# Moving batch 1's sums of q and k from the front of a fused attention and MoE kernel into its first matmul block

## Chip, cores and metric

One core of a Trainium2 chip runs the whole program. The metric is the device time of one execution in microseconds; the number of a kernel is the median of its runs. Each kernel also has one profiled execution, from which all rows below come.

## What is computed

The reference takes q, k and v of shape (4, 8, 576, 64), that is batch, heads, tokens, head size, and two sets of weights. The attention is a dense one on tokens pooled by four (144 of 576) plus one in a band of seven tokens; its result, as 2304 rows of 512, goes through a gated layer (inner width 1536) and a second one (inner width 2048).

```python
q_d = q.reshape(B, H, Sd, factor, D).mean(axis=3)
k_d = k.reshape(B, H, Sd, factor, D).mean(axis=3)
v_d = v.reshape(B, H, Sd, factor, D).mean(axis=3)
out_d = sm_attn(q_d, k_d, v_d)
out_up = np.repeat(out_d, factor, axis=2)
mask = np.abs(pos[:, None] - pos[None, :]) < factor
...
return (out_up + out_local).astype(np.float32)
...
return (silu * val @ w_out).astype(np.float32)
...
g = h * relu6 / 6.0
return (g @ w_out).astype(np.float32)
```

## The kernel before

**Blocks and units.** The 2304 tokens are cut into five blocks (`BLOCKS`, line 30). Block 0 has 512 columns, nearly all of batch 0. A block runs 68 units in a fixed order (line 152 and on): G and V (gate and value products, 12 matmuls each), O (the product with w_out), then H and P of the second layer. Units come in pairs: G0 G1 V0 V1 G2 G3 V2 V3 O0 O1 G4 G5 V4 V5 O2 O3 and so on. A pair shares one tile `wr` of split weights. In the first block the number m of a unit is its place in this list: G2 is m = 4, G5 is m = 11, O3 is m = 15.

**Weights.** In block 0 they come as 64-bit floats, one DMA of 512 KB for a unit on SP's queue (line 219). ScalarE takes the upper bits (`top`, line 236), VectorE joins the rest into fp32 (`w`, line 245), ScalarE and VectorE split that into a high and a low part (`wr`, lines 263 and 268), and ScalarE's queue stores the fp32 pair to DRAM for the later blocks (`kept`, line 251). Four raw buffers rotate, so that SP's next load waits for a line 245 four units back. `prefetch` (line 273) gives each step its lead in units.

**The front.** `first_batch` (line 362) does all of batch 0's attention before the first G, in an order written by hand: the string `FRONT` (line 46), whose words are steps on PE, VectorE and ScalarE.

**Batch 1's sums.** The second block needs batch 1's attention, which runs beside block 0. Its pooled q and k are made by GpSimd (POOL). The last word of `FRONT`, `sums` (line 706), issues four DMAs that load two of four tokens each (q and k, two halves, into the tile `stage`, 288 KB each), then four that add the other two tokens onto them in the DMA (line 702), then four additions (line 716) into `dnq` and `dnk`. `stage` takes over the buffer (tag `x2`) of `held`, the softmax of the front, so the first load waits for the last reader of `held`. `sums_T` (line 329) then transposes dnq and dnk on PE in four steps of four (`pqT_0`, `pqT_1`, `pkT_0`, `pkT_1`, line 336), ScalarE copies each to `qdT` or `kdT` (line 347), and the first dense scores of batch 1 (`pS`) use these in the H units. The loop over units takes one step of this at every odd m above 8 (line 1144).

**Order.** PE, VectorE and ScalarE work off their own lists in order. Program order is not the final order: unless an instruction is pinned, a scheduler may put it elsewhere on its engine. It put `pqT_0`, in the program after unit O1 (m = 9), between G2 and G3.

**Band scores.** `first_half` (line 1096) spreads VectorE's products `pr` (line 839) and their reductions `sc` (line 842) for batch 1's band over the units with m from 0.

Of the kernel before, what the change touches and what calls it, by code (L numbers as in the profile page):

```python
# [11 lines left out]
F32 = mybir.dt.float32  # L12
F32R = mybir.dt.float32r
# [6 lines left out]
ALU = mybir.AluOpType  # L20
AX = mybir.AxisListType

P = 128
# [16 lines left out]

SMALL = 384
SUMV = 25
FILL_P = (4, 4, 4, 4, 4, 0)


# [3 lines left out]
SC0 dM1 M0 Rk3 dE1 Rk2 dT0 dP0 W0 SC1 dS3 dM3 dT1 dP1 SC2 M1 dE3 W1 dS2 dT3 N0 dM2 dP3 SC3 dE2 dT2  # L49
PT0 M2 to0 N1 M3 dP2 to1 de0 Pd0 W3 dO0 dO3 dN0 dN3 dO2 N3 dO1 Pa0 W2 dN2 dN1 to2 PT1 Pa1 Pd1 SC5  # L50
SC4 M5 od0 W5 od1 PT3 V1 M4 N2 Pa3 de1 Xh1 W4 V0 Xh0 Pd3 Xl1 N5 PT2 V3 Pd2 Pa2 Xl0 hi0 PT5 Xh3 N4
Pd5 Pa5 Xl3 to3 V2 Xh2 PT4 de2 Xl2 Pd4 Pa4 de3 V5 lo0 Xh5 V4 Xh4 Xl5 Xl4 hi1 to4 lo1 sums
"""


# [1 line left out]
def tile_kernel(  # L57
# [12 lines left out]
    nc = tc.nc  # L70

    B, H, S, D = q.shape
# [5 lines left out]
    NJH = NJ // 2  # L78
    W = 7
    NC = DM // P  # L80
    F1 = w_gate.shape[1] // P
    F2 = w2_in.shape[1] // P
    UT = 4 * NSEG
# [4 lines left out]
    UMAX = max(BLOCKS)  # L88
# [6 lines left out]
    sp = ctx.enter_context(tc.tile_pool(name="sp", bufs=2))  # L95
# [15 lines left out]
    consts = cp.tile([P, SMALL // 4], F32, name="consts")  # L111
# [65 lines left out]
    NU = len(units) // NB  # L177
    NU1 = 3 * F1
# [133 lines left out]
    dn, qk = {}, {}  # L312

    def down_sums(b, kinds, gate=None):
        if gate is not None:
            tc.keep_in_program_order(nc.gpsimd.tensor_copy(consts[:gate.shape[0], 60:61], gate))
        for ws in kinds:
            for t in range(4):
                for w in ws:
                    if t == 0:  # L320
                        dn[w] = sp.tile([NJH, 2, H, D], F32, tag="dn" + w, name=f"dn{w}{b}", bufs=1)
                    src = {"q": q, "k": k, "v": v}[w]
                    for half in range(2):
                        tok = src[b, :, half * NJH * 4:(half + 1) * NJH * 4, :].rearrange("h (j t) d -> j t h d", t=4)
                        how = {"accum_op": ALU.add} if t else {}
                        tc.keep_in_program_order(nc.gpsimd.dma_start(dn[w][:, half], tok[:, t], **how))
                    yield

    def sums_T(b):
        for w in "qk":  # L330
            for hc in range(2):
                pt = bank("pa", f"p{w}T{b}_{hc}")[:, :2 * NJ].rearrange("p (c j) -> p c j", c=2)
                for cc in range(2):
                    c = 2 * hc + cc
                    for half in range(2):
                        nc.tensor.transpose(
                            pt[:, cc, half * NJH:(half + 1) * NJH],
                            dn[w][:, half, 2 * c:2 * c + 2, :].rearrange("j h d -> j (h d)"),
                            ident[:NJH, :NJH],
                        )  # L340
                yield w, hc, pt
# [20 lines left out]
    def first_batch():  # L362
# [7 lines left out]
        with tc.tile_pool(name="fp", bufs=1) as fp:  # L370
# [5 lines left out]
            first = {  # L376
                "fdpd": fp.tile([NJH, 2, 2, NJ], F32, tag="fdpd", name="fdpd_0", bufs=3),
                "fdpT": fp.tile([NJH, 2, NJ], F32, tag="fdpT", name="fdpT_0", bufs=8),
            }
# [123 lines left out]
            def fill(ps, n):  # L503

                for _ in range(n):
                    pe.matmul(ps[:, :2 * P], spin[:, :P], spin, start=True, stop=True)
# [140 lines left out]
            def PT(i):  # L647
                for hh in range(2):
                    ps = bank(f"acc{2 + hh}", f"fPT{i}_{hh}")
                    if not hh:  # L650
                        fill(ps, FILL_P[i])
                    ps = ps[:WK, :4 * QT].rearrange("p (h s) -> p h s", h=4)
# [35 lines left out]
                    to = columns(bi, col, xv)  # L688
                    vec.tensor_tensor(to[:, :, 1], xv, to[:, :, 0].bitcast(F32), op=ALU.subtract)

            twos = {}

            def pairs(t):
                for w, src in (("q", q), ("k", k)):
                    for half in range(2):
                        if not t:
                            st = stage[0][:, len(twos)]
                            twos[w, half] = st.rearrange("p (h t d) -> p h t d", h=H, t=2)
                        tok = src[1, :, half * NJH * 4:(half + 1) * NJH * 4, :]
                        tok = tok.rearrange("h (j t) d -> j h t d", t=4)[:, :, t:t + 2]  # L700
                        how = {"accum_op": ALU.add} if t else {}
                        tc.keep_in_program_order(nc.gpsimd.dma_start(twos[w, half], tok, **how))

            stage = []

            def sums():
                st = sp.tile([P, NC, 2, UMAX * UT], F32R, tag="x2", name="stage", bufs=1).bitcast(F32)
                stage.append(st.rearrange("p c a t -> p (c a t)")[:NJH].rearrange("p (n e) -> p n e", n=4))
                pairs(0)
                pairs(2)  # L710
                for w in "qk":
                    dn[w] = sp.tile([NJH, 2, H, D], F32, tag="dn" + w, name=f"dn{w}1", bufs=1)
                    for half in range(2):
                        st = twos[w, half]
                        tc.keep_in_program_order(
                            nc.gpsimd.tensor_tensor(dn[w][:, half], st[:, :, 0], st[:, :, 1], op=ALU.add)
                        )

            def od(n):
                for i in ((1, 0), (3, 2, 5, 4))[n]:  # L720
                    join_od(i)
# [11 lines left out]
            def lo(i):  # L733
# [2 lines left out]
            others = {  # L736
                "dS": dS, "dM": dM, "dE": dE, "dT": dT, "dP": dP, "dO": dO,
                "dN": dN, "SC": SC, "M": M, "W": W, "N": N, "PT": PT,
                "Pa": Pa, "Pd": Pd, "V": V, "Xh": Xh, "Xl": Xl, "sums": sums,
                "od": od, "to": to, "de": de, "hi": hi, "lo": lo,  # L740
            }
            for step in FRONT.split():
                name, *arg = re.match(r"([A-Za-z]+?)([qk]?)(\d*)$", step).groups()
                if name in ("T", "E", "R"):
                    w, at = arg
# [107 lines left out]
    def chunk_exp(b, c, n):  # L853
        sc, _ = pes[b, c]

        tc.keep_in_program_order(nc.scalar.activation(sc, sc, AF.Exp, scale=0.125))
# [129 lines left out]
    state = {}  # L986
# [102 lines left out]
    for bi in range(NB):  # L1089
        mine = chunks[at:at + len(CUTS[bi])]  # L1090
        at += len(mine)
        limit = starts[bi + 2] if bi + 2 <= NB else 0

        db = bi + 1 if bi + 1 < B else None

        def first_half():
            for m, ch in enumerate(mine):
                for _ in chunk_scores(*ch):
                    yield
                load_ahead(at - len(mine) + m + 3 if m + 3 <= len(mine) else loaded)  # L1100
            for _ in range(VAL0.get(bi, 0)):
                unit_values()
                yield

        def weigh(ch):
            chunk_exp(*ch)
            vq.extend((*ch, i) for i in range(ch[2]))

        def second_half():
            for ch in mine[1:] if bi in VAL0 else mine:  # L1110
                weigh(ch)
            while vq:
                unit_values()
                yield

        gens = [first_half(), second_half()]
        sizes = [sum(CUTS[bi]) + VAL0.get(bi, 0), sum(CUTS[bi]) - VAL0.get(bi, 0)]
        main = iter(())
        sums = iter(())
        if db:  # L1120
            sums = down_T(db, dn, qk)
            if bi:
                sums = chain(down_sums(db, ["qk", "v"], state["os"][:, (UMAX // 2 - 2) * DM:][:, :1]), sums)
        for i in range(bi * NU, (bi + 1) * NU):
            m = i - bi * NU
            prefetch(i)
            if m in CLOAD:
                load_ahead(at - len(mine) + min(CLOAD.index(m) + 1, len(mine)))
            if m == EXP_AT and bi in VAL0:
                weigh(mine[0])  # L1130
            run_unit(i)
            ph = 0 if m < NU1 else 1
            if m == NU1:
                for _ in gens[0]:
                    pass
                for _ in sums:
                    pass
                if db:
                    main = down_main(db, dn, qk)
            lo_, n_ = (0, NU1 - 2) if ph == 0 else (NU1, NU - NU1 - 6)  # L1140
            mm_ = m - lo_
            for _ in range(sizes[ph] * (mm_ + 1) // n_ - sizes[ph] * mm_ // n_ if mm_ < n_ else 0):
                next(gens[ph], None)
            if m % 2 and (bi or m > 8):
                next(sums, None)
            next(main, None)
            if m == NU - EARLY:
                load_ahead(at + 1)
            if i == SUMV:
                last = [t for key, t in state.items() if key[0] == "g"][-1]  # L1150
                for _ in down_sums(1, ["v"], last[:, 0, :1].bitcast(F32)):
                    pass
            step_x(limit)
            next_tick()
        if bi + 1 < NB:
            for _ in gens[1]:
                pass
            for _ in main:
                next_tick()
            while x_done[0] < starts[bi + 2]:  # L1160
                step_x(limit)
                next_tick()
# [30 lines left out]
```

## Time and profile before

| | us |
|---|---|
| median of 3 runs | 969.19 (968.88 to 971.98) |
| the profiled execution, own time | 970.18 |
| its span, first to last instruction | 968.4 |
| PE busy (matmuls) | 932.7 (96%) |
| VectorE (DVE) busy | 730.6 (75%) |
| ScalarE (ACT) busy | 504.2 (52%) |
| GpSimd (POOL) busy | 105.5 (11%) |

The span is the profiled execution's time from its first to its last instruction. Times in the rows below count from the start of the span. A bracket at the end of a row is the time for which the engine had stood idle before it and what released it. L with a number is the line of the kernel.

### The profile page before, as it was taken

How to read it: one execution, taken by the hardware profiler on the slowest of the kernel's cores; microseconds unless marked ns; L12 is line 12 of the kernel's file. 1: busy time of each engine (PE TensorE's matmuls, PEld its weight loads, DVE VectorE, ACT ScalarE, POOL GpSimd, SP SyncE). 2: the span in 40 equal slices, each digit the busy share in tenths (PEclk: the TensorE clock that was granted, in tenths of full speed). 3: DMA queues.
4: the chain of work that ended last, by engine and by line, in shares of the span. 5: the costliest groups of instructions: out<-in, count | busy, mean ns of one | idle time of the engine just before them, and what ended most of it. 6: DMA issues, size and time to landing. Idle time of an engine off the chain costs nothing.

```text
span 968.4 us, 13032 instructions
## 1 busy us (share of the span) xinstructions
PE 932.7 (96%) x4848; PEld 789.6 (82%) x4848; DVE 730.6 (75%) x1066; ACT 504.2 (52%) x942; POOL 105.5 (11%) x117
## 2 busy tenths in 40 slices
PE   8876999999899999999999999999999999999997
PEld 5765887777799988888888778888888788999996
DVE  5857985799879988999764799997337994445652
ACT  4863565975544567553334764443335445434542
POOL 7032002100044300015420000000000000000000
PEclk8997999999999999999999999999999999999999
DMA  9589899667699922359972211463232323433331
GB/s 220 166 277 265 288 338 344 183 202 255 244 269 271 187 91 88 109 185 243 220 146 87 88 66 66 161 209 109 88 108 87 105 91 102 159 131 123 122 126 32
DMA packets 100263, 161.08 MB, mean 166 GB/s; under 512 B 53440, under 2 KB 57152, under 8 KB 100200
## 3 DMA queue, kind: packets, MB, share of 16 engines
q1 hardware_dynamic: 57680, 131.43, 41.2%
q0 software_dynamic: 37408, 10.71, 10.2%
q10 hardware_dynamic: 5112, 18.12, 4.7%
q8 instruction: 38, 0.62, 0.3%
q14 instruction: 25, 0.20, 0.1%
HBM read 137.31 MB, written 22.54 MB: 165 GB/s over the span
## 4 chain that ended last, share of the span: by engine, by line
PE 76%; DVE 13%; DMA 5%; issue 3%; ACT 2%; SPq 1%; POOL 0%; ACTq 0%; DVEq 0%
PE pH L357 16%; PE aP L1034 16%; PE pV L357 13%; PE aO L1034 12%; PE pG L357 12%; DVE wr L268 3%; DMA stage<-in_q_dram 3%; DVE pv L876 2%; DVE xf L905 1%; PE pS L930 1%; DMA w<-in_moe_w_in_dram 1%; DVE h L1008 1%; PE pO L780 1%; DVE pv L880 1%; PE fPT L153 1%
## 5 line engine op out<-in xcount | busy, mean ns | idle before, releaser
L268 DVE TENSOR_TENSOR wr<-w,wr 128x1024 fp32r<-128x1024 f32 x170 | 208.4, 1226 | 125.2 <-ACT wr L263 125.0
L263 ACT ACTIVATE wr<-w 128x1024 fp32r<-128x1024 f32 x170 | 179.6, 1057 | 119.6 <-issue 59.7
L357 PE MATMUL pH<-x,wr 128*128 128x512 f32 (+1 forms) x960 | 212.8, 372 | 0.0
L1034 PE MATMUL aP<-wr,gH 128*128 128x512 f32 x864 | 211.6, 395 | 0.3 <-ACT gH L1009 0.3
L357 PEld LDWEIGHTS pH<-x,wr 128*128 128x128 f32 x960 | 172.8, 188 | 25.8 <-issue 2.9
L1034 PEld LDWEIGHTS aP<-wr,gH 128*128 128x128 f32 x864 | 159.6, 188 | 34.9 <-issue 2.5
L357 PE MATMUL pG<-xr,wr 128*128 128x512 f32 (+1 forms) x720 | 155.1, 370 | 1.5 <-ACT xr L153 1.0
L357 PE MATMUL pV<-xr,wr 128*128 128x512 f32 (+1 forms) x720 | 153.8, 368 | 1.2 <-ACT sl L998 1.2
L1034 PE MATMUL aO<-gV,wr 128*128 128x512 f32 (+1 forms) x720 | 152.8, 368 | 0.0
L357 PEld LDWEIGHTS pG<-xr,wr 128*128 128x128 f32 x720 | 131.9, 189 | 19.2 <-ACT xr L153 1.2
L357 PEld LDWEIGHTS pV<-xr,wr 128*128 128x128 f32 x720 | 130.8, 188 | 18.7 <-ACT sl L998 2.0
L1034 PEld LDWEIGHTS aO<-gV,wr 128*128 128x128 f32 x720 | 130.8, 188 | 16.9 <-DVE gV L1010 0.2
L1007 ACT ACTIVATE h<-pH,consts 128x512 f32<-128x512 f32 (+1 forms) x80 | 51.4, 643 | 59.6 <-PE pH L357 59.3
L1009 ACT ACTIVATE gV<-sl 128x512 fp32r<-128x512 f32 (+1 forms) x60 | 35.0, 584 | 84.4 <-DVE sl L1004 84.4
L998 ACT ACTIVATE sl<-pG 128x512 f32<-128x512 f32 (+1 forms) x60 | 33.3, 554 | 71.5 <-PE pG L357 71.4
L839 DVE TENSOR_TENSOR pr<-q,k 128x1792 f32<-128x1792 f32 x27 | 54.5, 2020 | 14.7 <-DMA k<-in_k_dram 14.5
L1009 ACT ACTIVATE gH<-h 128x512 fp32r<-128x512 f32 (+1 forms) x80 | 46.9, 586 | 31.3 <-DVE h L1008 31.0
L1008 DVE SCALAR_TENSOR_TENSOR h<-h,pH 128x512 f32<-128x512 f32 (+1 forms) x80 | 50.5, 631 | 15.1 <-ACT h L1007 14.6
L236 ACT ACTIVATE top<-w 128x512 f16<-128x512 bf16 x68 | 51.9, 790 | 16.8 <-DMA w<-in_moe_w_in_dram 6.2
L1010 DVE TENSOR_TENSOR gH<-h,gH 128x512 fp32r<-128x512 f32 (+1 forms) x80 | 50.5, 632 | 10.7 <-ACT gH L1009 10.3
L245 DVE SCALAR_TENSOR_TENSOR w<-w,top 128x512 int32<-128x512 int32 x68 | 45.5, 684 | 13.3 <-ACT top L236 11.2
L876 DVE TENSOR_TENSOR pv<-sc,v 128x1792 f32<-128x1792 f32 x27 | 54.6, 2021 | 0.5
(131 smaller groups left out, 749.0 us busy)
## 6 DMA issues: line engine op xcount, KB each, us to landing
w<-kept SPq DMA_DIRECT2D x136, 512.0 KB
kept<-w ACTq DMA_DIRECT2D x34, 512.0 KB
w<-in_moe_w_out_dram SPq DMA_DIRECT2D x28, 512.0 KB
w<-in_moe_w_in_dram SPq DMA_DIRECT2D x16, 512.0 KB
w<-in_moe_w_gate_dram SPq DMA_DIRECT2D x12, 512.0 KB
w<-in_moe_w_val_dram SPq DMA_DIRECT2D x12, 512.0 KB
out_dram<-os SPq DMA_DIRECT2D x16, 256.0 KB
dnv<-in_v_dram POOLq DMA_DIRECT2D x24, 144.0 KB, 8.1
```

The lines of the kernel that those rows point to most:

```text
L236: behind(nc.scalar.activation(halves(top[i % 2], 2, F16)[:, :, 1], h3.bitcast(BF16), AF.Copy))
L245: behind(nc.vector.scalar_tensor_tensor(w32[i // 2][:, i % 2].bitcast(I32), h12, 13, top[i % 2], op0=ALU.logical_shift_right, op1=ALU.bitw ...
L263: behind(nc.scalar.activation(parts[i][:, 0], w32[i // 2].rearrange("p u e -> p (u e)"), AF.Copy))
L268: behind(nc.vector.tensor_tensor(r[:, 1], s, r[:, 0].bitcast(F32), op=ALU.subtract))
L357: nc.tensor.matmul(ps, r[:, a, c], x[:, c, b_, :ps.shape[1]], start=part is HIGH and a == c == 0, stop=part is LOW and c == NC - 1,)
L839: nc.vector.tensor_tensor(pr, qt[:, a:a + SUB, None, :].to_broadcast([P, SUB, W, D]), win(kt, a, SUB), op=ALU.mult)
L876: nc.vector.tensor_tensor(pr, pe[:, a:a + SUB, :, None].to_broadcast([P, SUB, W, D]), win(vt, a, SUB), op=ALU.mult)
L1007: nc.scalar.activation(h, ps, AF.Relu, scale=1 / 6, bias=half1[:, 0:1])
L1008: nc.vector.scalar_tensor_tensor(h, h, 1.0, ps, op0=ALU.min, op1=ALU.mult)
L1009: nc.scalar.activation(g[:, 0, :nt], h, AF.Copy)
L1010: nc.vector.tensor_tensor(g[:, 1, :nt], h, g[:, 0, :nt].bitcast(F32), op=ALU.subtract)
L1034: nc.tensor.matmul(ps, **one, start=f_ == 0 and a == b_ == 0, stop=f_ == nf - 1 and b_ == 1,)
```

## The change

The word `sums` leaves `FRONT`, and its work is cut in two. After unit G2 (m = `SUMP` = 4) POOL copies one value of the newest g tile, which is `gV_1`, to a place that nobody reads, and then issues the eight DMAs: since POOL works in order, they wait for ScalarE's write of `gV_1`. After unit G5 (m = `SUMJ` = 11) it copies a value of `gV_3` and makes the four additions. The four steps of transposes come at odd m above 14 in place of 8, that is behind O3, G7, V7 and O5. The band scores of block 0 are spread over the units from m = 3 in place of 0. Nothing else is computed, and no DMA is added; two copies of one element are.

```diff
+SUMP, SUMJ = 4, 11
...
-... Xh5 V4 Xh4 Xl5 Xl4 hi1 to4 lo1 sums
+... Xh5 V4 Xh4 Xl5 Xl4 hi1 to4 lo1
...
+    def gate_on(tile_):
+        gate = tile_[:, 0, :1].bitcast(F32)
+        tc.keep_in_program_order(nc.gpsimd.tensor_copy(consts[:, 60:61], gate))
+
+    def pair_sums():
+        st = sp.tile([P, NC, 2, UMAX * UT], F32R, tag="x2", name="stage", bufs=1).bitcast(F32)
+        st = st.rearrange("p c a t -> p (c a t)")[:NJH].rearrange("p (n e) -> p n e", n=4)
+        for t in (0, 2):
+            for i, (w, src) in enumerate((("q", q), ("k", k))):
+                for half in range(2):
+                    if not t:
+                        twos[w, half] = st[:, 2 * i + half].rearrange("p (h t d) -> p h t d", h=H, t=2)
+                    tok = src[1, :, half * NJH * 4:(half + 1) * NJH * 4, :]
+                    tok = tok.rearrange("h (j t) d -> j h t d", t=4)[:, :, t:t + 2]
+                    how = {"accum_op": ALU.add} if t else {}
+                    tc.keep_in_program_order(nc.gpsimd.dma_start(twos[w, half], tok, **how))
+
+    def join_pairs():
+        for w in "qk":
+            dn[w] = sp.tile([NJH, 2, H, D], F32, tag="dn" + w, name=f"dn{w}1", bufs=1)
+            for half in range(2):
+                st = twos.pop((w, half))
+                tc.keep_in_program_order(
+                    nc.gpsimd.tensor_tensor(dn[w][:, half], st[:, :, 0], st[:, :, 1], op=ALU.add)
+                )
...
-            def sums():
...
-                pairs(0)
-                pairs(2)
...
-            lo_, n_ = (0, NU1 - 2) if ph == 0 else (NU1, NU - NU1 - 6)
+            first = 0 if bi else 3
+            lo_, n_ = (first, NU1 - 2 - first) if ph == 0 else (NU1, NU - NU1 - 6)
...
+            if bi == 0 and m in (SUMP, SUMJ):
+                gate_on([t for key, t in state.items() if key[0] == "g"][-1])
+                (pair_sums if m == SUMP else join_pairs)()
-            if m % 2 and (bi or m > 8):
+            if m % 2 and (bi or m > SUMJ + 3):
                 next(sums, None)
```

The order of the instructions shows three things. First PE at the start of block 0, before the change (pG, pV and aO are the products of units G, V and O):

```order
L357 MATMUL pV_1_998<-xr_767,wr_899 128x512 x12
L357 MATMUL pG_2_1021<-xr_767,wr_944 128x512 x12
L336 MATMUL pqT_0_1158<-ident,dnq_912 128x72 x4
L357 MATMUL pG_3_1043<-xr_767,wr_944 128x512 x12
L357 MATMUL pV_2_1070<-xr_767,wr_995 128x512 x12
```

PE now goes from pG_2 straight to pG_3. The transposes stand further on in its list, from the end of unit O3:

```order
L1035 MATMUL aO_3_1115<-gV_3_1102,wr_1176 128x512
L365 MATMUL pqT_0_1290<-ident,dnq_1195 128x72 x4
L386 MATMUL pG_6_1302<-xr_767,wr_1228 128x512 x12
L386 MATMUL pG_7_1324<-xr_767,wr_1228 128x512 x12
L365 MATMUL pqT_1_1339<-ident,dnq_1195 128x72 x4
L386 MATMUL pV_6_1351<-xr_767,wr_1270 128x512 x12
L386 MATMUL pV_7_1375<-xr_767,wr_1270 128x512 x12
L365 MATMUL pkT_0_1392<-ident,dnk_1198 128x72 x4
```

Before, pkT_1 stood where pqT_0 stands now. Then POOL between the front and block 0's end, now (fvd is the front's value tile):

```order
L475 TENSOR_TENSOR fvd<-vd_243 72x4x64
L334 COPY consts<-gV_1_996 128x1
L347 DMA stage<-in_q_dram 72x8x128 x2
L347 DMA stage<-in_k_dram 72x8x128 x2
...
L334 COPY consts<-gV_3_1102 128x1
L355 TENSOR_TENSOR dnq_1195<-stage 72x512 x2
L355 TENSOR_TENSOR dnk_1198<-stage 72x512 x2
L317 COPY consts<-gV_9_1530 128x1
L327 DMA dnv_1535<-in_v_dram 72x8x64 x8
```

The two rows L334 are new; before, the DMAs of stage followed the row of fvd and the additions followed the DMAs. Last, ScalarE at the same place, before the change:

```order
L998 ACTIVATE sl_2_1034<-pG_2_1021 128x512
L1009 ACTIVATE gV_1_1011<-sl_1_960 128x512
L347 ACTIVATE qdT_1156<-pqT_0_1158 128x288
L263 ACTIVATE wr_1040<-w_8_1019 128x1024
L998 ACTIVATE sl_3_1056<-pG_3_1043 128x512
```

The row of qdT is gone from here in the changed kernel, and the split of w_8 follows gV_1 directly. VectorE's first `pr` stands where it stood, behind w_8 and ahead of gV_0, although the scores now begin at m = 3. From G4 to the end of block 0 some forty rows of VectorE and of ScalarE change places with their neighbours; behind block 0 only two stores of results move, by one place on SP.

## Rows read from the trace of the kernel before

**Rows 1.** Chain of waits that ended last, 47 to 100 us: start, length, what.

```profile
52.77 8.23 DMA stage<-in_q_dram
...
62.87 17.12 DMA stage<-in_q_dram
80.05 1.27 POOL dnq L716
```

**Rows 2.** Timeline of PE, 40 to 190 us: start, length, instruction, idle before.

```profile
66.07 2.88 PE L357 MATMUL pG<-xr,wr 128*128 128x512 f32 x12
79.05 0.38 PE L336 MATMUL pqT<-ident,dnq 72*128 72x72 f32 x1 [10.10 <-POOL dnq L716]
81.36 0.62 PE L336 MATMUL pqT<-ident,dnq 72*128 72x72 f32 x3 [1.93 <-POOL dnq L716]
81.73 4.33 PE L357 MATMUL pG<-xr,wr 128*128 128x512 f32 x12
85.89 5.61 PE L357 MATMUL pV<-xr,wr 128*128 128x512 f32 x24
91.34 5.60 PE L1034 MATMUL aO<-gV,wr 128*128 128x512 f32 x24
...
102.23 0.41 PE L336 MATMUL pqT<-ident,dnq 72*128 72x72 f32 x4
102.45 5.72 PE L357 MATMUL pV<-xr,wr 128*128 128x512 f32 x24
...
113.78 0.41 PE L336 MATMUL pkT<-ident,dnk 72*128 72x72 f32 x4
```

**Rows 3.** Timeline of DVE, 44 to 190 us.

```profile
71.71 2.03 DVE L839 TENSOR_TENSOR pr<-q,k 128x1792 f32<-128x1792 f32 x1 [6.86 <-DMA k<-in_k_dram]
...
74.25 1.22 DVE L268 TENSOR_TENSOR wr<-w,wr 128x1024 fp32r<-128x1024 f32 x1
...
83.41 1.34 DVE L268 TENSOR_TENSOR wr<-w,wr 128x1024 fp32r<-128x1024 f32 x1 [3.61 <-ACT wr L263]
87.46 1.33 DVE L245 SCALAR_TENSOR_TENSOR w<-w,top 128x512 int32<-128x512 int32 x2 [2.71 <-ACT top L236]
...
96.35 1.22 DVE L268 TENSOR_TENSOR wr<-w,wr 128x1024 fp32r<-128x1024 f32 x1
```

**Rows 4.** Timeline of SP's queue, 51 to 66 us: issues.

```profile
59.26 0.51 SPq L141 DMA_DIRECT2D k<-in_k_dram  x1
```

**Rows 5.** Timeline of ACT, 44 to 110 us.

```profile
76.10 0.63 ACT L1009 ACTIVATE gV<-sl 128x512 fp32r<-128x512 f32 x1 [6.51 <-DVE sl L1004]
```

**Rows 6.** Timeline of POOL, 60 to 330 us.

```profile
77.43 1.56 POOL L716 TENSOR_TENSOR dnq<-stage 72x512 f32<-72x512 f32 x1 [9.89 <-DMA stage<-in_q_dram]
...
89.05 1.29 POOL L716 TENSOR_TENSOR dnk<-stage 72x512 f32<-72x512 f32 x1 [5.38 <-DMA stage<-in_k_dram]
143.15 0.72 POOL L316 COPY consts<-gV 128x1 f32<-128x1 f32 x1 [52.81 <-ACT gV L1009]
```

**Rows 7.** DMA queues, 51 to 92 us: packets, MB, share of 16 engines (q0 is POOL's).

```profile
q1 hardware_dynamic: 2507, 6.93, 49.4%
q0 software_dynamic: 3584, 2.37, 36.9%
q10 hardware_dynamic: 801, 2.95, 18.4%
```

**Rows 8.** DMA queues, 143 to 183 us, while POOL loads dnv.

```profile
q0 software_dynamic: 4635, 1.15, 28.3%
```

**Rows 9.** Stretches: engines' busy us (xcount), PE clock, DMA share, GB/s.

```profile
69.00:84.00 15.00, 3.02 (x9) 2.35 (x10) 8.69 (x9) 2.57 (x5) 4.10 (x3) 0.56 1.22 293
90.00:120.00 30.00, 30.00 (x142) 24.79 (x140) 30.00 (x32) 16.87 (x26) 0.34 (x1) 1.00 0.79 271
...
143.00:180.00 37.00, 36.00 (x162) 28.69 (x161) 23.95 (x35) 23.95 (x36) 10.69 (x9) 1.00 1.10 349
...
186.00:260.00 74.00, 71.09 (x356) 55.55 (x356) 68.25 (x115) 50.99 (x100) 0.00 (x0) 1.00 0.63 215
```

More of the change, by code (lines that the diff above doesn't have):

```diff
@@ L51 @@
 SC4 M5 od0 W5 od1 PT3 V1 M4 N2 Pa3 de1 Xh1 W4 V0 Xh0 Pd3 Xl1 N5 PT2 V3 Pd2 Pa2 Xl0 hi0 PT5 Xh3 N4
-Pd5 Pa5 Xl3 to3 V2 Xh2 PT4 de2 Xl2 Pd4 Pa4 de3 V5 lo0 Xh5 V4 Xh4 Xl5 Xl4 hi1 to4 lo1 sums
+Pd5 Pa5 Xl3 to3 V2 Xh2 PT4 de2 Xl2 Pd4 Pa4 de3 V5 lo0 Xh5 V4 Xh4 Xl5 Xl4 hi1 to4 lo1
 """
@@ L327, in down_sums @@
                     yield
+    twos = {}
+    def gate_on(tile_):
[21 more added lines that the diff above has]
+                )
     def sums_T(b):
@@ L689, in Xl @@
                     vec.tensor_tensor(to[:, :, 1], xv, to[:, :, 0].bitcast(F32), op=ALU.subtract)
[L691 to L704, printed above, removed]
-            def sums():
-                st = sp.tile([P, NC, 2, UMAX * UT], F32R, tag="x2", name="stage", bufs=1).bitcast(F32)
-                stage.append(st.rearrange("p c a t -> p (c a t)")[:NJH].rearrange("p (n e) -> p n e", n=4))
-                pairs(0)
-                pairs(2)
[L711 to L717, printed above, removed]
             def od(n):
@@ L738, in first_batch @@
                 "dN": dN, "SC": SC, "M": M, "W": W, "N": N, "PT": PT,
-                "Pa": Pa, "Pd": Pd, "V": V, "Xh": Xh, "Xl": Xl, "sums": sums,
+                "Pa": Pa, "Pd": Pd, "V": V, "Xh": Xh, "Xl": Xl,
                 "od": od, "to": to, "de": de, "hi": hi, "lo": lo,
@@ L1139, in tile_kernel @@
                     main = down_main(db, dn, qk)
-            lo_, n_ = (0, NU1 - 2) if ph == 0 else (NU1, NU - NU1 - 6)
+            first = 0 if bi else 3
+            lo_, n_ = (first, NU1 - 2 - first) if ph == 0 else (NU1, NU - NU1 - 6)
             mm_ = m - lo_
-            for _ in range(sizes[ph] * (mm_ + 1) // n_ - sizes[ph] * mm_ // n_ if mm_ < n_ else 0):
+            for _ in range(sizes[ph] * (mm_ + 1) // n_ - sizes[ph] * mm_ // n_ if 0 <= mm_ < n_ else 0):
                 next(gens[ph], None)
-            if m % 2 and (bi or m > 8):
+            if bi == 0 and m in (SUMP, SUMJ):
+                gate_on([t for key, t in state.items() if key[0] == "g"][-1])
+                (pair_sums if m == SUMP else join_pairs)()
+            if m % 2 and (bi or m > SUMJ + 3):
                 next(sums, None)
```

## The prediction, made before the changed kernel had run

> **What bounds the kernel now.** I read the page first. PE is busy for 932.7 of 968.4 us, so most of the time is matmuls that the change does not touch; only the 36 us in which PE is not busy, and the matmuls that run slowly behind a stand, can be won. The page's chain of waits gives 3% of the span to the DMAs of stage, the one item there that is neither an engine's work nor spread over the program. So the second view is that chain, from 47 to 100 us [rows 1]: it leaves the engines at 52.77 us, passes through two transfers of stage (8.23 and 17.12 us) and one addition on POOL, and comes back to PE.
>
> The third view is PE's timeline at that place [rows 2]. G2 starts at 66.07. Then PE stands for 10.10 us until half of dnq is there, does one transpose, stands for 1.93 us, does three more, and runs G3. V2 starts at 85.89. The stand has a second price: over 69 to 84 us the granted clock is 0.56 in the mean [rows 9], that is, mostly the lower of the two levels, 1.2 GHz, after PE had stopped. G3 takes from 81.73 to 85.89, 4.16 us, where a unit at the full 2.4 GHz takes 2.725 (V2 and V3 from 85.89 to 91.34).
>
> The fourth view is VectorE's timeline [rows 3], since PE could only go on if the next weights are split. VectorE stood three times between 64 and 88 us: 6.86 us for the k tile of the first band scores, 3.61 for ScalarE's split of w_8, which stood behind the copy of pqT_0 in ScalarE's order, and 2.71 for ScalarE again. From 90 to 120 it works 30.00 of 30 us [rows 9].
>
> The fifth are the DMA queues [rows 7]. From 51 to 92 us the eight transfers of stage take 36.9% of 16 engines, 15.1 us of 41, for 2.37 MB. The other two queues move 9.88 MB in 67.8%, 27.8 us.
>
> **What the change does, part by part.**
>
> *The transposes leave the place between G2 and G3.* From the start of G2 to that of V2 it is 85.89 - 66.07 = 19.82 us; two units at full clock take 5.45. That gives 14.37. pqT_0 is still done later, at 0.22 us in a running stream (102.23 to 102.45 [rows 2]): 14.15 remain. The other three steps only move and cost the same.
>
> *What V2 would wait for next.* V2 would now start at 71.52. Its weights are split by VectorE at 74.25 to 75.47, 3.95 us too late, because VectorE hung on the k tile until 71.71 [rows 3]. That tile was issued at 59.26 [rows 4], while stage was in flight; now it is not. Ahead of it and with it lie one weight unit (512 KB), q (128 x 768 fp32 values, 384 KB), k itself (128 x 1152, 576 KB) and a store of a split pair (512 KB), 2.0 MB. At the 355 GB/s of the other queues in their own time (9.88 MB in 27.8 us) that is 5.7 us, so my estimate is a landing at 65 and a VectorE that is 6.7 us earlier. The wait is then 0. Ends: 0, and 3.95 if k lands as before.
>
> *The gate and the two copies.* POOL's queue holds nothing else there, so nobody waits behind the first copy but the sums. The copy took 0.72 us where it was already used [rows 6]. ScalarE ended gV_1 at 76.73 [rows 5]; 6.7 earlier is 70.0, so the first DMA goes out at 70.7 in place of 52.77. From the first issue to the end of the second dnq addition it was 80.05 + 1.27 - 52.77 = 28.55 us [rows 1]: dnq is ready at 99.3. PE gets to pqT_0 27.45 us after V2's start (85.89 to 113.78, less two steps of 0.22 that are no longer in it [rows 2]): at 99.0. The wait is 0.3. For dnk it was 90.34 - 52.77 = 37.6 us [rows 6], that is 108.3, and PE reaches pkT_0 at 110.3: no wait. Ends: 0, and 7 if the gate opens no earlier than before (106.0 against 99.0). The second gate, gV_3, is long past by then and costs nothing.
>
> *Stage beside a PE at full pace.* This is the cost that nothing in the old trace shows. Stage now runs from about 71 to 108 us. There PE needs weights at the rate of 90 to 120 us: a DMA share of 0.79 with PE at 30.00 of 30 [rows 9]. Stage adds 15.1 of 37.6 us, 0.40: 1.19 in all. The nearest row is 143 to 180, where POOL loads dnv in nearly the same way (4635 packets for 28.3% [rows 8], stage 3584): the engines showed 1.10 and PE worked 36.00 of 37. An excess of 0.09 over 37.6 us is 3.4 us of DMA time, or 4.3 us of PE's pace. Against it stands a lead: the split for V4 ended at 97.57, V4 started at 102.45, so 4.9 us. Not all of it is free, as VectorE is full there. I take 3 us lost. Ends: 0 if the lead covers it, 6.8 if the engines only give the 1.05 of 51 to 92 us (0.14 of 37.6 us over 0.79).
>
> *VectorE in less time.* To follow a PE 14.15 us earlier it must be 14.15 - 4.9 = 9.3 earlier; its three stands sum to 13.2, and each was an effect of stage or of PE's stand. Cost 0; if only the first goes, the gain is held to 6.86 + 4.9 = 11.8.
>
> *The rest.* Band scores from m = 3: VectorE's first product keeps its place, so nothing. dnv's gate is gV_9 at 143 [rows 6], behind the additions by far. The reordered neighbours up to the end of block 0: nothing, to within 1 us either way.
>
> Sum: 14.15 - 0 - 0.3 - 3 = 10.8 us. The profiled execution took 970.18 us and the median is 969.19, 0.99 below it; the gain is a stretch of the trace that any run has, so I take it off the median: **958.4 us**.
>
> **The rivals.** What a measurement of this kernel can tell from no change is 0.3%, 2.9 us.
>
> *The whole stand is won (0.12).* The lead covers the contention: 969.19 - 14.15 = 955.0. For it: PE lost only about 1 us in 143 to 180. Against it: stage is 0.40 of the engines, dnv 0.28.
>
> *The wait comes back at a new place (0.17).* k lands no earlier, V2 waits 3.95, and PE reaches pqT_0 at 102.9 with dnq ready at 106.0: 3.1 more. If the second stand also drops the clock, one unit costs 4.16 - 2.73 = 1.4: the gain is 5.7, 963.5 us. For it: even my own two times, 99.3 and 99.0, leave no margin on a path of 28.55 us that now has a busier PE beside it. The Trainium skill has a rule that speaks against the change here, in DMA: Bandwidth & Descriptors, Rules for kernel authors: a DMA should be issued early and its semaphore waited on late. By that rule alone the later issue is a loss and this rival the forecast; no trace here shows the later issue yet.
>
> *The gain is lost before block 0 ends (0.09).* VectorE works 68.25 of 74 us from 186 to 260 [rows 9], and PE cannot leave the block before it. If VectorE spends the 14 us as more idle time in 143 to 180, where it already stands for 13 of 37, the end stays: 969.2. Against it: those stands are waits for data that would also come earlier.
>
> *Slower (0.07).* POOL's accumulating transfers crowd out the weights in 71 to 108 us. At a rate r of the other queues PE, which uses them at 271 GB/s [rows 9], falls behind by 37.6 x (1 - r/271) less the lead of 4.9. To lose 17 us (14.15 and 2.9) r must be under 113 GB/s; at 80 it is 21.6 lost, 976.6 us. For it: a byte of stage costs 2.3 times as much of the engines as one of the others (15.1 us for 2.37 MB, 27.8 for 9.88 [rows 7]). Against it: the others still had 9.88 MB in 41 us, 241 GB/s, beside the very same transfers.
>
> **How the numbers follow.** The forecast has 0.55, for gains from 8 to 13 us. With the two rivals that win something it is 0.84 for faster by over 0.3%; 0.09 for within 0.3%; 0.07 for slower. The range runs from the whole stand, with half a us of scatter, 954.5, to the wait that comes back with the contention's worse end beside it: 966.5. It leaves out the last two rivals and little else.
>
> **What would show it.** Right: no row of PE waiting for dnq between G2 and G3, V2 at about 71.5, pr on VectorE at 65 to 67 in place of 71.71, a PE clock of 1.00 from 52 us on, stage issued at 70 to 71, O3's end at 99 to 103. Wrong: a stand of over 3 us of PE at pqT_0 (the sums are late), PE waiting for splits or for gV between G4 and O3 (the weights are late), or a gain at O3 that is gone at the start of block 1.

## The result, and the profile after

| | before | after |
|---|---|---|
| median, us (4 runs each) | 970.59 (968.88 to 972.41) | 961.46 (959.84 to 961.97) |
| ratio | | 0.9903, interval 0.9877 to 0.9929 |
| span of the profiled execution | 968.4 | 958.1 |
| PE busy | 932.7 | 931.1 |
| VectorE busy | 730.6 | 730.6 |
| POOL busy | 105.5 | 108.9 |

The kernel is faster by 9.1 us of medians. Of the 10.3 us between the two spans, 9.2 lie in block 0: from its first product to the first of block 1 it took 272.28 - 54.49 = 217.79 us, now 261.76 - 53.18 = 208.58. Another 1.3 lie before block 0 and are scatter (0.2 are lost again behind it): the experiments below leave the front as it is, but for POOL's issues in e1 and e11, and their block 0 began anywhere from 52.99 to 55.55 us. So from here on I compare lengths from that first product.

PE's timeline after, the piece that answers to [rows 2]:

```profile
64.77 2.88 PE L386 MATMUL pG<-xr,wr 128*128 128x512 f32 x12
68.53 3.02 PE L386 MATMUL pG<-xr,wr 128*128 128x512 f32 x12 [0.87 <-DVE sl L1005]
71.38 5.60 PE L386 MATMUL pV<-xr,wr 128*128 128x512 f32 x24
...
82.26 5.60 PE L386 MATMUL pG<-xr,wr 128*128 128x512 f32 x24
92.83 7.85 PE L386 MATMUL pV<-xr,wr 128*128 128x512 f32 x24 [4.97 <-ACT sl L999]
100.53 5.61 PE L1035 MATMUL aO<-gV,wr 128*128 128x512 f32 x24
105.97 0.42 PE L365 MATMUL pqT<-ident,dnq 72*128 72x72 f32 x4
```

The stand for dnq between G2 and G3 is gone: V2 starts at 71.38, 18.20 us behind the block's start in place of 31.40. But there is a new stand, which no step of the sum named: 4.97 us ahead of V4, for ScalarE, and then 7.85 us for 24 matmuls that take 5.60 elsewhere. The stretches show why they are slow:

```profile
69.00:84.00 15.00, 15.00 (x68) 12.40 (x67) 15.00 (x17) 7.79 (x11) 6.78 (x7) 1.00 1.01 327
90.00:120.00 30.00, 27.16 (x118) 22.21 (x119) 28.32 (x30) 16.27 (x26) 7.65 (x4) 0.89 0.97 276
93.00:96.00 3.00, 3.00 (x8) 2.32 (x9) 3.00 (x3) 1.89 (x3) 0.78 (x1) 0.50 1.28 262
96.00:99.00 3.00, 3.00 (x12) 2.40 (x11) 3.00 (x4) 1.09 (x2) 1.28 (x1) 0.77 1.12 353
```

(Columns as in [rows 9].) Over 69 to 84 us the clock is now 1.00 where it was 0.56. Instead it is 0.50, the lower level of 1.2 GHz, from 93 to 96, right behind PE's stand, while the DMA engines show 1.28.

What PE waited for is ScalarE's `sl_4`, which empties G4's bank. ScalarE's own timeline:

```profile
89.32 0.77 ACT L237 ACTIVATE top<-w 128x512 f16<-128x512 bf16 x1 [8.12 <-DMA w<-in_moe_w_out_dram]
91.57 0.78 ACT L237 ACTIVATE top<-w 128x512 f16<-128x512 bf16 x1 [1.48 <-DMA w<-in_moe_w_gate_dram]
92.21 0.57 ACT L999 ACTIVATE sl<-pG 128x512 f32<-128x512 f32 x1
```

and the chain of waits there:

```profile
74.59 16.90 DMA w<-in_moe_w_gate_dram
...
91.57 0.41 ACT top L237
...
92.21 0.58 ACT sl L999
...
92.83 7.17 PE pV L386 x21
```

G4 had ended by 85.2, and V4's own weights were split by 82.5. But ScalarE works in order, and its list had the copies `top_15` and `top_16`, for the units O3 and G6, ahead of `sl_4` (the rows at 89.32 and 91.57). Both waited for raw weights still on their way; w_16 took 16.90 us to land.

POOL, and on VectorE the first band product, the split for V4 and V5, and one later row:

```profile
69.89 1.86 POOL L347 DMA_DIRECT2D stage<-in_q_dram  x2 [0.17 <-issue]
79.03 1.42 POOL L347 DMA_DIRECT2D stage<-in_q_dram  x1 [5.68 <-DMA stage<-in_q_dram]
101.51 1.28 POOL L355 TENSOR_TENSOR dnq<-stage 72x512 f32<-72x512 f32 x1 [4.22 <-DMA stage<-in_q_dram]
103.27 2.64 POOL L355 TENSOR_TENSOR dnk<-stage 72x512 f32<-72x512 f32 x1 [0.48 <-DMA stage<-in_k_dram]
```

```profile
64.11 2.02 DVE L840 TENSOR_TENSOR pr<-q,k 128x1792 f32<-128x1792 f32 x1 [0.57 <-DMA k<-in_k_dram]
...
81.23 1.22 DVE L269 TENSOR_TENSOR wr<-w,wr 128x1024 fp32r<-128x1024 f32 x1
...
104.69 1.77 DVE L1011 TENSOR_TENSOR gV<-sl,gV 128x512 fp32r<-128x512 f32 x1
```

`pr` starts at 64.11 in place of 71.71 [rows 3]. The second dnq addition ends at 102.79, and PE comes to pqT_0 only at 105.97, so this wait is not seen.

### The profile page after: what moved, and what is told of

Its sections match the earlier page's. It is cut to its first block, busy times and chain, and to the rows that moved or that the text cites. A ratio compares the mean times of both kernels' runs of the same rounds, so it can differ in the third digit from the quotient of the medians.

```text
span 958.1 us, 13046 instructions
## 1 busy us (share of the span) xinstructions
PE 931.1 (97%) x4848; PEld 788.8 (82%) x4848; DVE 730.6 (76%) x1066; ACT 503.5 (53%) x942; POOL 108.9 (11%) x119
## 3 DMA queue, kind: packets, MB, share of 16 engines
q10 hardware_dynamic: 5112, 18.12, 4.7%
## 4 chain that ended last, share of the span: by engine, by line
PE 75%; DVE 11%; DMA 5%; issue 3%; ACT 3%; SPq 1%; ACTq 0%; DVEq 0%
PE pH L386 18%; PE aP L1035 18%; PE pG L386 12%; PE aO L1035 11%; PE pV L386 11%; DVE wr L269 3%; DMA w<-in_moe_w_gate_dram 2%; DMA k<-in_k_dram 1%; DVE w L246 1%; PE pS L931 1%; DVE pv L877 1%; PE pO L781 1%; DMA kept<-w 1%; SPq L142 1%; DMA w<-in_moe_w_in_dram 1%
## 5 line engine op out<-in xcount | busy, mean ns | idle before, releaser
L1035 PEld LDWEIGHTS aO<-gV,wr 128*128 128x128 f32 x720 | 130.8, 188 | 16.9 <-DVE gV L1011 0.2
L840 DVE TENSOR_TENSOR pr<-q,k 128x1792 f32<-128x1792 f32 x27 | 54.5, 2019 | 10.3 <-DMA k<-in_k_dram 10.2
```

The lines of the kernel that those rows point to most:

```text
L840: nc.vector.tensor_tensor(pr, qt[:, a:a + SUB, None, :].to_broadcast([P, SUB, W, D]), win(kt, a, SUB), op=ALU.mult)
L1035: nc.tensor.matmul(ps, **one, start=f_ == 0 and a == b_ == 0, stop=f_ == nf - 1 and b_ == 1,)
```

## The experiments

Twelve kernels ran, in three groups: e1, e3, e5 and e6; e4, e8, e9 and e11; and the last four. Each ratio is to the kernel before as it ran in the same group (medians 971.19, 971.60 and 973.08 us), so across groups the ratios compare better than the medians. Below, "block 0" is its length in the kernel's profiled execution, first product to first product of block 1, with its three pieces: to V2, from V2 to H0, from H0 to the end. A single execution scatters by about 1 us there (the changed kernel twice: 208.58 and 207.69).

| kernel | block 0 | to V2 | V2 to H0 | H0 to end | median | ratio to before, interval |
|---|---|---|---|---|---|---|
| before | 217.79 | 31.40 | 83.88 | 102.51 | 970.59 | 1 |
| after | 208.58 | 18.20 | 90.36 | 100.02 | 961.46 | 0.9903, 0.9877 to 0.9929 |
| after again | 207.69 | 18.28 | 90.15 | 99.26 | 960.73 | 0.9875, 0.9850 to 0.9900 |
| e1 early issue | 211.30 | 27.34 | 83.00 | 100.96 | 963.66 | 0.9918, 0.9899 to 0.9938 |
| e3 no accumulating | 207.38 | 18.36 | 89.48 | 99.54 | 959.59 | 0.9876, 0.9859 to 0.9894 |
| e4 scores from 0 | 209.15 | 18.38 | 91.45 | 99.32 | 960.54 | 0.9885, 0.9863 to 0.9907 |
| e5 spread | 217.65 | 18.19 | 94.55 | 104.91 | 970.88 | 0.9987, 0.9970 to 1.0004 |
| e6 top later | 210.46 | 18.12 | 86.69 | 105.65 | 962.86 | 0.9916, 0.9891 to 0.9941 |
| e8 no transfers | 201.24 | 18.09 | 82.97 | 100.18 | 953.73 | 0.9813, 0.9786 to 0.9839 |
| e9 sl first | 208.03 | 18.15 | 90.62 | 99.26 | 963.15 | 0.9913, 0.9888 to 0.9937 |
| e11 before, end order | 216.00 | 32.67 | 83.01 | 100.32 | 968.85 | 0.9964, 0.9944 to 0.9984 |
| e12 both | 206.78 | 18.11 | 85.72 | 102.95 | 959.94 | 0.9875, 0.9841 to 0.9910 |
| e13 later only | 208.21 | 19.59 | 88.18 | 100.44 | 962.43 | 0.9898, 0.9870 to 0.9925 |
| e14 gate on gV_0 | 207.24 | 18.69 | 89.26 | 99.29 | 959.94 | 0.9867, 0.9842 to 0.9893 |

**What do stage's transfers cost at the new place?** No transfers at all:

```diff
-                    tc.keep_in_program_order(nc.gpsimd.dma_start(twos[w, half], tok, **how))
+                    if not t:
+                        tc.keep_in_program_order(nc.gpsimd.memset(st[:, 2 * i + half], 1.0))
```

> Leaves out all eight transfers of stage; POOL fills stage with ones in their place, so batch 1's sums of q and k are not computed. Theory A: w_15 and w_16 land in time, V4 neither waits nor runs slowly, 7 us less than the changed kernel in block 0 (201 to 203 us in place of 208.6), 953 to 956. Rival C (VectorE, POOL or ScalarE hold V4 whatever the transfers do): V4 waits 3 us or more, 959 to 962.

ScalarE and PE in this kernel:

```profile
84.54 0.80 ACT L237 ACTIVATE top<-w 128x512 f16<-128x512 bf16 x1 [2.01 <-DMA w<-in_moe_w_gate_dram]
85.20 0.57 ACT L1000 ACTIVATE sl<-pG 128x512 f32<-128x512 f32 x1
```

```profile
87.62 5.60 PE L387 MATMUL pV<-xr,wr 128*128 128x512 f32 x24
```

w_16, issued at 74.46, lands by 84.5: 10.0 us in place of 16.9. V4 does not wait, no matmul is slow, and all of the gain stays to the end of the block: 208.58 - 201.24 = 7.3 us. That is the price of stage's transfers beside a PE at full pace (6.5 us against the second execution of the changed kernel; by medians 6.8 against e4, which ran beside e8 and behaves as the changed kernel does). Theory A holds.

Then half of them, without the four that accumulate:

```diff
-        for t in (0, 2):
+        for t in (0,):
```

> Leaves out the four accumulating transfers of stage, so batch 1's sums of q and k lack half of their tokens. Theory A: half of stage's load is gone, w_16 lands well before 91, PE's wait at V4 falls from 4.97 us to under 1.5 and the slow clock behind it goes: 954 to 958. Rival C (VectorE and POOL in each other's way, or VectorE's order, hold the weights, not the transfers): the wait at V4 stays at 3 us or more and the time at 959 to 962.

Here theory A missed: V4 still waits 3.32 us, V4 and V5 then take 8.43 for their 24 matmuls, and block 0 is 207.38. The chain of waits, and PE:

```profile
77.13 15.24 DMA w<-in_moe_w_gate_dram
...
92.45 0.41 ACT top L237
```

```profile
93.72 8.43 PE L386 MATMUL pV<-xr,wr 128*128 128x512 f32 x24 [3.32 <-ACT sl L999]
```

w_16 takes 15.24 us, so of the 6.9 us by which stage delays it the four plain transfers make 5.2. In the changed kernel they go out at 69.89 to 73.4, just ahead of w_16 and beside the next band tiles; the accumulating ones follow from 79.03 on, each when its plain one has landed, and add only 1.7. I read this so: the wait hangs less on how much stage moves than on what of it is in flight when a weight with no slack goes out. Rival C's numbers came (3.32 us and 959.59), but not its cause, VectorE or POOL's additions: e8 keeps both, the additions from 80.53 to 87.5, and has no wait.

**Is the later issue itself the loss?** The Trainium skill, in DMA: Bandwidth & Descriptors, Rules for kernel authors, would issue early and wait late. So the DMAs go back to the end of the front, and only their use stays late:

```diff
-V5 lo0 Xh5 V4 Xh4 Xl5 Xl4 hi1 to4 lo1
+V5 lo0 Xh5 V4 Xh4 Xl5 Xl4 hi1 to4 lo1 sums
...
-            if bi == 0 and m in (SUMP, SUMJ):
+            if bi == 0 and m == SUMJ:
...
-                (pair_sums if m == SUMP else join_pairs)()
+                join_pairs()
```

> The changed kernel, but stage's eight transfers are issued where the kernel before issued them (at the end of the front, about 53 us); additions and transposes stay late. Theory A (the price of the change is stage's transfers beside the weights from 72 to 108 us): V4 no longer waits 4.97 us and runs at full clock, 7.2 us won; but the k tile lands at about 71 again, VectorE loses 6.9 us, V2 waits about 4 us and one or two units run slowly: within 2 us of the changed kernel, 960 to 964. Rival B (issue early, wait late: the later issue was itself the mistake): at least 5 us faster than the changed kernel, 953 to 957.

VectorE, and PE:

```profile
71.79 2.03 DVE L840 TENSOR_TENSOR pr<-q,k 128x1792 f32<-128x1792 f32 x1 [7.49 <-DMA k<-in_k_dram]
```

```profile
76.21 5.24 PE L386 MATMUL pG<-xr,wr 128*128 128x512 f32 x12 [7.80 <-DVE sl L1005]
81.29 5.63 PE L386 MATMUL pV<-xr,wr 128*128 128x512 f32 x24
```

The k tile comes late behind stage, VectorE stands for 7.49 us, PE for 7.80, and G3 is slow: V2 comes 9.1 us later than in the changed kernel. From V2 to H0 it then takes 83.00, as with no transfers. Block 0 is 2.7 us longer than after's; its median is the higher one too (963.66 against 961.46), though the intervals of the two ratios overlap. Theory A gave the time (it had expected 4 us at V2, and 7.80 came at G3). Rival B falls: e1 is not 5 us faster, since both places cost, the early one as much or a little more. Seen from the kernel before, e1 moves the use alone and has 6.5 of the 9.2 us of block 0 already (4.9 of 6.7 without the block's end), in a ratio of 0.9918; moving the issue as well adds 2.7 in these two traces, and no difference of times that is clear of noise. So most of this change's gain is that PE no longer waits early. Of that rule the late wait is borne out here, and the early issue is not.

**Spreading the transfers over more units.**

```diff
-SUMP, SUMJ = 4, 11
+SUMP = {4: (0, "q"), 8: (0, "k"), 13: (2, "q"), 17: (2, "k")}
+SUMJ = 20
...
-                (pair_sums if m == SUMP else join_pairs)()
+                pair_sums(*SUMP[m]) if m in SUMP else join_pairs()
```

> Same transfers, spread: q's first pair behind gV_1, k's first pair behind gV_3, q's second pair and k's second pair behind gV_5, additions behind gV_7 and the transposes between units after that. Theory A: fewer of stage's bytes beside the weights at any time, so V4's wait falls from 4.97 us to under 1.5 us: 955 to 959. Rival D (the engines have no room for stage anywhere while block 0 streams raw weights): as many us are lost at later places, by 130 us: 960 to 963.

```profile
88.96 5.74 PE L389 MATMUL pV<-xr,wr 128*128 128x512 f32 x24 [1.30 <-ACT sl L1002]
...
127.17 0.80 PE L389 MATMUL pV<-xr,wr 128*128 128x512 f32 x1 [5.27 <-ACT sl L1002]
129.31 8.01 PE L389 MATMUL pV<-xr,wr 128*128 128x512 f32 x23 [1.35 <-DVE wr L270]
```

At V4 the wait falls to 1.30, as theory A said. But PE stands at V8 instead, 5.27 and 1.35 us, and runs slowly there: from V2 to H0 it is 94.55 in place of 90.36. So rival D is right about the place, and both missed the time, which is that of the kernel before: the block's end takes 5 us more as well, where VectorE again waits for a store, as the part on the end of the block tells.

**ScalarE's order.** Two runs put `sl_4` ahead of the copy for w_15 and `sl_5` ahead of that for w_16. e6 also moves VectorE's decodes of the two and the split for O2 in the program; e9 moves only the two copies (`keep_in_program_order` pins an instruction behind what the program wrote before it on its engine):

```diff
+PINNED = (10, 11)
...
-            behind(nc.scalar.activation(halves(top[i % 2], 2, F16)[:, :, 1], h3.bitcast(BF16), AF.Copy))
+            ins = nc.scalar.activation(halves(top[i % 2], 2, F16)[:, :, 1], h3.bitcast(BF16), AF.Copy)
+            (tc.keep_in_program_order if i - LA in PINNED else behind)(ins)
...
             run_unit(i)
+            if i in PINNED:
+                decode_a(i + LA)
```

> ScalarE's copies for w_15 and w_16 are put behind sl_4 and sl_5 in its order; no transfer moves. Theory A (sl_4 was ready and stood in order behind a copy that waited for w_16): V4 starts within 1 us of G5's end, and PE waits 1 to 4 us at O2 instead, whose weights include w_15: 957.5 to 961. Rival E (V4 waited for something of its own, its weights or VectorE): the wait before V4 stays at 4 us or more and the time at 961 or above.

> The changed kernel with two copies pinned in ScalarE's order: the one for w_15 behind sl_4, the one for w_16 behind sl_5. VectorE's order at the end of block 0 stays that of the changed kernel. Theory A (ScalarE's order, not the load alone, makes the 4.97 us at V4): V4 starts within 1 us of G5's end, at full clock; O2 waits 1 to 3 us for its split; from the first product of block 0 to that of block 1 it is 203 to 206 us in place of 208.6, and the time 956 to 959.5. Rival D (the load must be paid somewhere, or VectorE's end of the block takes it): V4's wait gone but 207 us or more, 960 to 963.

PE in e9 (V5, which waits 0.47 us, then pqT_0 and G6):

```profile
91.06 3.03 PE L388 MATMUL pV<-xr,wr 128*128 128x512 f32 x12 [0.47 <-ACT sl L1001]
...
99.37 0.23 PE L367 MATMUL pqT<-ident,dnq 72*128 72x72 f32 x1
104.90 0.62 PE L367 MATMUL pqT<-ident,dnq 72*128 72x72 f32 x3 [5.30 <-POOL dnq L357]
105.26 6.94 PE L388 MATMUL pG<-xr,wr 128*128 128x512 f32 x24
```

In both the wait at V4 is gone without a transfer moved. So the late weight and ScalarE's order made it together: taking away either one ends it (e8, e9). But in e9 PE then stands 5.30 us at pqT_0, for the sums, and G6 and G7 are slow (6.94 us). The two waits lay side by side, and the one at V4 hid the one at pqT_0, though not at that length: in e9 the second dnq addition ends at 104.84, 2.05 us later than in the changed kernel. Neither run won time. Theory A was right about the cause in both and missed block 0 and the time (208.03 and 963.15 in e9, 962.86 in e6); in e9 O2 did not wait, and block 0 is where rival D had it. In e6 PE waits 1.5 us at O2 and 1.3 at pqT_0; by H0 it has won 3.7 us against the changed kernel, and the block's end loses 5.6.

**Both ends at once.** e13 takes the transposes two units later each and pins VectorE's decode of w_66 behind the block's last sum `o` (why, the part on the end of the block tells); e12 does both and pins the copies as e9 does; e14 pins the copies and issues stage one g tile earlier (`SUMP` = 2). The changed kernel ran again beside them.

```diff
-            if m % 2 and (bi or m > SUMJ + 3):
+            if m % 2 and (bi or m > SUMJ + 5):
```

> The changed kernel as it is, as the measure for the three beside it. All theories: 959.5 to 962.5, block 0 within 1 us of 208.6, 4 to 5.5 us of waiting at V4.

> The changed kernel with its four transposes two units later each and w_66 behind o at the block's end; ScalarE's order stays. Theory J (two parallel ends, the late weights at V4 and the late sums at pqT_0, of which the first hides the second): nothing won, V4 still waits 4 us or more, 207.5 to 210 us for block 0, 960 to 963. Rival D (the transposes' place matters by itself): 205 us or less, 956 to 958.

> sl_4 and sl_5 ahead of the copies for w_15 and w_16, and the four transposes two units later, w_66 behind o at the block's end. Theory J: with both ends gone PE waits less than 1 us in all between V2 and H0, block 0 takes 201.5 to 204.5 us, 953.5 to 957. Rival D (stage's load is paid at whatever place comes next): a third wait of 3 us or more before H0 or at the block's end, 206.5 us or more, 958.5 to 963.

> sl_4 and sl_5 ahead of the two copies, transposes where the change has them, and stage's transfers behind gV_0 in place of gV_1, 4 to 6 us earlier. Theory J: the sums of q are ready that much earlier, pqT_0 waits under 1.5 us in place of 5.3, block 0 takes 202.5 to 205.5 us, 954.5 to 958. Rival D: the weights of V4 or O2 are that much later, 206.5 us or more, 958.5 to 963.

The changed kernel repeats: 960.73, and 4.89 us of waiting at V4. e13 wins nothing, as theory J has it (962.43), though V4 waits 3.34 us there and not 4 or more; G3 waits 2.25 in place of 0.87. In e12 PE goes from V2 to H0 in 85.72 us, 4.4 less than after again, with waits of under 0.5 us each (1.6 in all, where theory J had under 1). The longest of them, and two behind H0:

```profile
106.03 0.41 PE L367 MATMUL pqT<-ident,dnq 72*128 72x72 f32 x3 [0.44 <-POOL dnq L357]
...
159.99 3.02 PE L388 MATMUL pH<-x,wr 128*128 128x512 f32 x10 [1.56 <-ACT x L1050]
...
234.15 0.41 PE L899 MATMUL px<-ident,o 128*128 128x128 f32 x2 [0.95 <-DVE o L885]
```

But 3.7 of it are given back from H0 on, of which the two later waits are 2.5; block 0 comes out at 206.78, and the median (959.94) cannot be told from after again (960.73). In e14 PE does not wait at pqT_0, as theory J had it, but stands at V5, for `sl_5`, which stood behind the copy for w_15:

```profile
94.35 5.49 PE L388 MATMUL pV<-xr,wr 128*128 128x512 f32 x12 [3.26 <-ACT sl L1001]
```

```profile
91.06 0.78 ACT L238 ACTIVATE top<-w 128x512 f16<-128x512 bf16 x1 [4.77 <-DMA w<-in_moe_w_out_dram]
```

So theory J is right about the two ends and wrong that nothing lies behind them; in block 0 and in time both e12 and e14 came out where rival D had them (206.5 us or more, 958.5 to 963). Of the 7.3 us that stage costs, none of these orders gets back more than about 1 against after again. Of the 3.7 us by which e12's end of the block is longer, PE's idle time is 2.4 and its busy time 1.3 (100.30 against 98.98); why, I did not settle.

**The end of the block.** 2.5 of the 9.2 us come from behind H0. VectorE before, at the last sum `o` of the block, and PE, which stood 2.12 us for it:

```profile
254.55 0.68 DVE L881 TENSOR_TENSOR pv<-pv 128x512 f32<-128x512 f32 x1
257.22 0.69 DVE L245 SCALAR_TENSOR_TENSOR w<-w,top 128x512 int32<-128x512 int32 x1 [1.99 <-DMA kept<-w]
257.83 1.22 DVE L268 TENSOR_TENSOR wr<-w,wr 128x1024 fp32r<-128x1024 f32 x1
258.96 0.42 DVE L882 TENSOR_TENSOR o<-pv 128x256 f32<-128x256 f32 x1
```

```profile
259.53 0.41 PE L896 MATMUL px<-ident,o 128*128 128x128 f32 x2 [2.12 <-DVE o L882]
```

The decode of w_66 stands ahead of `o` and waits for a store. In the changed kernel the scheduler had put VectorE's list there in a slightly different order, and the wait did not come:

```profile
246.56 0.68 DVE L882 TENSOR_TENSOR pv<-pv 128x512 f32<-128x512 f32 x1
247.16 0.68 DVE L246 SCALAR_TENSOR_TENSOR w<-w,top 128x512 int32<-128x512 int32 x1
247.76 0.41 DVE L883 TENSOR_TENSOR o<-pv 128x256 f32<-128x256 f32 x1
```

e11 is the kernel before with that one instruction pinned behind `o`:

```diff
-            behind(nc.vector.scalar_tensor_tensor(
+            (tc.keep_in_program_order if i == 66 else behind)(nc.vector.scalar_tensor_tensor(
```

> The kernel before, with one VectorE instruction moved: the decode of w_66, which stood ahead of the last sum o of the block and waited 1.99 us for the store of an earlier pair, now stands behind it. Theory H (2.5 us of the change's 9.2 in block 0 come from VectorE's order at the block's end, which the change altered only by chance): PE's 2.12 us at px shrink to under 0.7, block 0 takes 214.5 to 216.5 us in place of 217.8, the time falls by 1.5 to 3 us against before. Rival I (the 2.5 us belong to the earlier sums): less than 1 us against before, 217 us or more.

PE at the same place in e11:

```profile
255.98 0.41 PE L896 MATMUL px<-ident,o 128*128 128x128 f32 x2
```

The wait of 2.12 us at the last px is gone; another, at the px before it, stays (0.80, before 0.75). From H0 to the end it takes 100.32, 2.2 less than before, and the ratio of 0.9964 is a gain of 3.5 us (1.6 to 5.4 by its interval). Theory H holds for 2.2 of the 2.5 us: this part has nothing to do with where the sums stand, and the kernel before could have had it alone. VectorE's wait for that store is in the traces of before (1.99), e5 (3.20) and e6 (2.03), and in none of the others; of the other kernels only e12 has as long an end of the block.

**The first scores.**

```diff
-            first = 0 if bi else 3
+            first = 0
```

> The changed kernel with the first scores asked for from the first unit again. Theory A (VectorE's first product keeps its place, so that part of the change does nothing): block 0 within 1.5 us of 208.6, 960 to 963. Rival G (the later scores are part of the gain): PE waits for a split or for VectorE by 2 us or more before V4, 964 to 967.

209.15 and 960.54: nothing, as the prediction had it.

## Why the prediction was right, point by point

- *The transposes leave their place: 14.15, and V2's next wait 0.* By V2 it should have been 14.37 (0.22 was for pqT_0, further on); measured 31.40 - 18.20 = 13.20. Of the 1.17 missing, 0.87 is the wait of G3 for a bank that VectorE empties, at a place where PE stood anyway before. The k tile: estimate 65, row 64.11.
- *The gate.* Issue predicted at 70.7, row 69.89. dnq predicted ready at 99.3, row 102.79: 33 us of path, not 28.55. The wait of 0.3 was 0 in the trace, but only because PE was late too, by luck; e9 shows 5.30 when PE is not. The rival of the wait that comes back had half of its mechanism, the late sums, hidden behind another wait; its other half, a late k tile, did not come.
- *Stage beside PE at full pace: 3 us, ends 0 and 6.8.* **This is the step that failed, by its size**: 7.3 us (e8; 6.5 by the second execution), at the worse end. I set an excess of DMA time, averaged over 37.6 us, against a lead of 4.9 us of V4's split. That lead was there (split by 82.5, V4 due at about 87.7) and was no help: what came late was w_16, the weight of G6, and ScalarE's order tied G4's `sl_4` to it. An average share says nothing of which transfer is late: without the accumulating half the three queues are at 0.87 from 70 to 110 us, no excess at all (1.05 in the changed kernel), and V4 still loses 3.32 us and 2.83 of slow matmuls. So that the worse end comes near in size is luck. And behind this stand the clock was at its lower level (0.50 at 93 to 96), which is 2.25 of the 7.3 us (7.85 - 5.60), which I had counted for the old stand and in a rival, not in this term.
- *VectorE in less time: 0.* Right: block 0's length fell although VectorE works 72.53 of 74 us in 186 to 260. The rival that the gain is lost by the block's end fell in the other direction.
- *The rest: nothing, within 1 us.* 2.5 us won at the block's end, 2.2 of which e11 gives by VectorE's order alone. An edit can bring that order by chance: the change did, e5 and e6 did not. This luck covers over half of the mis-sized step: 14.15 - 0.3 - 3 = 10.8 was forecast, 13.2 - 6.5 + 2.5 = 9.2 came (6.5 is the whole difference from V2 to H0, 90.36 against 83.88; before had 0.97 us of waiting of its own there).
- *The time and the range.* 961.46 is 3.1 us above the forecast: 1.7 of it is the smaller gain (9.1 of medians for 10.8), and 1.4 that the kernel before ran at 970.59 beside it, not 969.19. The range was narrower than its text says: 966.5 is the returning wait (963.5) with the 3 us of contention; with the worse end of 6.8 it would be 970.3.
- *Slower, by the accumulating transfers.* Fell with the time; and without them most of the loss at V4 stays (e3), so they are not what mainly crowds out the weights.
- *Signs.* No row of PE for dnq between G2 and G3: right. V2, `pr` and the issue came within 1 us of what was said (71.38, 64.11, 69.89). "A PE clock of 1.00 from 52 us on": wrong, 0.50 at 93 to 96. O3's end at 99 to 103: wrong, about 106. Of the signs of being wrong, late weights between G4 and O3 came, not as a wait for a split or gV but for `sl_4`.

## What to carry to other kernels

An engine that works in order ties everything behind a waiting instruction to the transfer that it waits for: before moving a bulk load, look in each list for the instruction that waits for data needed late and stands ahead of one needed now. Two late inputs can lie side by side; taking away the wait that the trace shows may only uncover the other, so ask what is ready when behind it. And where a scheduler makes the order, compare the order far from the edit too: about a quarter of this gain came from there.

## What the runs showed of the hardware

The queue of POOL's transfers, 70 to 110 us, after, and then without the four accumulating ones:

```profile
q0 software_dynamic: 3584, 2.37, 34.7%
```

```profile
q0 software_dynamic: 448, 1.18, 10.0%
```

The accumulating half takes 3136 packets for 1.19 MB, where the plain half takes 448 for 1.18, and 24.7% of the engines' time against 10.0%: 2.5 times as much for the same bytes, by the difference of the two kernels. I had priced all eight alike.

The additions on POOL took 1.28 to 2.64 us beside a full VectorE, and VectorE's `gV` at 104.69 took 1.77 us in place of 0.68 while one of them ran. The two slow each other, and the transfers are not needed for it. In e8, which has none:

```profile
80.53 3.99 POOL L356 TENSOR_TENSOR dnq<-stage 72x512 f32<-72x512 f32 x2
```

```profile
81.12 2.25 DVE L269 TENSOR_TENSOR wr<-w,wr 128x1024 fp32r<-128x1024 f32 x1
```

The split takes 2.25 us where it takes 1.22 elsewhere, and the additions 2.0 each; in e3 one that runs at 90.19, while VectorE stands, takes 1.26. Neither was on the path.
